# Loads of a retention-plus-feed-forward kernel issued in another order around its attention stretches

## The chip, the cores and the metric

The kernel runs on one core of a Trainium2 chip. Five engines work side by side, each through its own list of instructions in a fixed order: TensorE (PE, with its weight loads shown as PEld), VectorE (DVE), ScalarE (ACT), GpSimd (POOL) and SyncE (SP). SP does nothing here but issue transfers between the chip's main memory and the on-chip buffers: if one transfer must wait, every transfer behind it in SP's list waits too. The metric is the device time of one execution in microseconds (us); lower is better.

## The reference, cut to what matters

```python
scores = matmul(q, k.T) / sqrt(64)                  # q, k, v: 8 batches, 8 heads, 576 positions, 64 wide
ret    = matmul(scores * decay_per_head, v)         # decay gamma**(i-j) below the diagonal, 0 above
x      = ret as (4608 tokens, 512)
h      = x @ w_in                                   # 512 x 2048
out    = (h - tanh(h)) @ w_out                      # 2048 x 512
```

## The kernel before, in words

The 576 positions are cut into nine blocks of 64 positions, and a block n is worked on for all eight batches at once: 512 tokens. Retention is computed block by block with a running state. For two batches of a block (a turn) the function `attend` runs 128 small matmuls (64x64) on PE. The `attend` of one turn also computes the scores of the next one, so a turn's q and k (tile `qk`) must be loaded and q multiplied by a decay table (tile `qtab` or `work`, by POOL, `prep`) before the previous turn's `attend`; its v and rows of k (tile `vr`) must be loaded and v scaled (POOL again) before its own.

The feed-forward part is done in words: each fp32 operand is split into a high and a low word, and three fp32r matmuls replace one. `mm1(n, f)` computes one of 16 slices f of the hidden layer of block n, `mm2(n, f)` multiplies slice f by the second weight: 12 matmuls of 128x512. A hidden slice is written to main memory (`spill`) and read back (`fetch`, tile `s`, three buffers) some slices ahead of its `mm2`; ACT makes its high word `gh`, DVE its low word `gl` (`split`; for every third slice the tiles are `gs`).

The order of the program is:

- A first part converts the weights and does `mm1` of blocks 0 and 1.
- The late loop (k = 0 to 31) does `mm2` of blocks 1 and 0. `late[k + 4]` is fetched in step k, `resume` makes its tanh two steps later, `words` its words. In the same loop DVE makes sums of the first weight's slices (`sums`), ACT and SP store them to `wvar`, and `raw_words` stores 24 unchanged words of those slices (256 KB each), one per step for k = 6 to 29.
- A loop over f = 0 to 15 does `mm1(2, f)`.
- `stage_b(n, m0)` does `mm2` of an even block n (2, 4, 6, 8), f = 0 to 15. Before each even f it runs one `attend` of the turns of blocks n+1 and n+2: `attend(m0)` to `attend(m0 + 7)`. Here `attend(i)` means the i-th of the eight in its stage (0 to 7), on PE ahead of `mm2(n, 2i)`. At its end `attend` prepares tables (`prep_turn`) and issues the loads of coming turns (`load_turn`).
- `stage_a(n)` does the first matmul of two blocks with seven products in place of eight, from sums of x (tiles `xhv`, `xlv`, made by `put`) and the sums of weights in `wvar`, which `load_slot` brings in (tile `ws`, four products at a time). Stage B and stage A alternate: B(2), A(3), B(4), A(5), B(6), A(7), B(8).

Two tables of q (for two blocks) are loaded by `load_tables` into a part of tile `work`. A load into it may not start before POOL's last `prep` with the old tables has ended. The order of each engine's list is the order in which the code issues its instructions; nothing reorders it afterwards (`in_order`).

The lines of the profile that matter below: L297 the small matmuls, L445 `mm1`, L500 `mm2`, L898 the products of stage A, L929 `mm2` inside stage A; L470 `fetch`, L693 `raw_words`, L724 sums to `wvar`, L769 `load_tables`, L788 `load_turn`, L887 `load_slot`; L247 `prep` on POOL; L475 `resume`, L482 `words`, L913 and L914 `split`, L814 `put` of low words on DVE.

Of the kernel before, what the change touches and what calls it, by code (L numbers as in the profile page):

```python
# [9 lines left out]
F32 = mybir.dt.float32  # L10
F32R = mybir.dt.float32r
# [8 lines left out]
P = 128  # L20
NF = DF // P
# [16 lines left out]
FIRST = 3  # L38
# [33 lines left out]
def retention_ffn(ctx: ExitStack, tc: tile.TileContext, ins, out, spill, wvar):  # L72
    nc = tc.nc
# [392 lines left out]
    fetched = {}  # L466

    def fetch(n, f):
        fetched[n, f] = pool.tile([P, BLK], F32, tag="g", bufs=3, name=f"s{n}_{f}")
        nc.sync.dma_start(fetched[n, f], spill[n, f])  # L470
# [265 lines left out]
    for k, (n, f) in enumerate(late):  # L736
        if k in (3, 16, 29):
            follow, scale = entry3(first + (0, 2, 5)[(3, 16, 29).index(k)], rest)
        if 0 < k < len(late) - 1:
            words(*late[k + 1])  # L740
        if k < len(late) - 2:
            resume(*late[k + 2])
        if k + 4 < len(late):
            fetch(*late[k + 4])
        if k in (3, 16, 29):

            follow()
# [12 lines left out]
        if 6 <= k < 30:  # L760
            raw_words(*raws[k - 6])

    turns = [(c + u) * B + b for c in range(FIRST, NC, 2) for b in range(0, B, 2) for u in range(2)]
    def load_tables(c):

        both = work[:, 2].rearrange("p (n i s) -> p n i s", n=2, i=4)
        nc.sync.dma_start(both, qtab_d[c - 1 : c + 1].rearrange("n p i s -> p n i s"))  # L769
        for u in range(2):  # L770
            qtabs[c + u] = both[:, u]

    def load_turn(m, t):
        if m >= len(turns):
            return
        j = turns[m]
        c, b = divmod(j, B)
        if m == 1 and t == 0:
            load_qtab(c)
        if t == 0 and m and m % 8 == 0:  # L780
            load_tables(c)
# [6 lines left out]
        nc.sync.dma_start(part, qkv_d[c - 1, b : b + 2, :, 2 * t : 2 * t + 2].rearrange("u p t i s -> p u t i s"))  # L788
        parts[j, t] = part
        for u in range(2):  # L790
            loaded.setdefault(j + u, Parts([None, None])).parts[t] = part[:, u]

    def prep_turn(m, t):
        if m < len(turns):
            prep(turns[m], t)


# [10 lines left out]
    def put(v, b, src, sub):  # L808

        hi, lo = [x[:, :, b * C : (b + 2) * C].rearrange("p i (u t) -> p u i t", u=2) for x in xv[v]]  # L810
        if sub == 0:
            nc.scalar.copy(hi, src)
        else:
            nc.vector.tensor_tensor(lo, src, hi.bitcast(F32), op=ALU.subtract)  # L814
# [3 lines left out]
    def attend(m, between):  # L818

        j = turns[m]  # L820
        c, b = divmod(j, B)
        first, states = (c - FIRST) % 2 == 0, c < NC - 1
        if first and b == 0:
            new_xv()
        o = bank(f"own{j}", "own")
        outs, same = pair(m_out, j, o), []
        if states:
            new = bank(f"new{j}", "new")
            same += pair(m_state, j, new)
        more = m + 1 < len(turns)  # L830
        if more:
            sc = bank(f"s{turns[m + 1]}", "h")
            same = pair(m_score, turns[m + 1], sc) + same
        run(same, outs)
        if more:
            after_score(turns[m + 1], sc, 2)
        if first:
            a = pool.tile([P, 2, 4, C], F32, tag="cv", bufs=4, name=f"xa{j}")
            kept[b] = a
            put(0, b, o[:, :, 0:2], 0)  # L840
            put(5, b, o[:, :, 2:4], 0)
            nc.scalar.copy(a, o)
            if states:
                add_state(j, new)
            between()
            put(0, b, a[:, :, 0:2], 1)
            put(5, b, a[:, :, 2:4], 1)
        else:
            a = kept.pop(b)
            t13 = pool.tile([P, 2, 2, 2, C], F32, tag="cv", bufs=4, name=f"t13_{j}")  # L850
            t24 = pool.tile([P, 2, 2, 2, C], F32, tag="cv", bufs=4, name=f"t24_{j}")
            t1, t3, t2, t4 = t13[:, 0], t13[:, 1], t24[:, 0], t24[:, 1]
            own = pool.tile([P, 2, 4, C], F32, tag="cv", bufs=4, name=f"xb{j}")
            nc.scalar.copy(own, o)
            put(4, b, o[:, :, 2:4], 0)
            nc.vector.tensor_tensor(t3, own[:, :, 2:4], own[:, :, 0:2], op=ALU.subtract)
            nc.gpsimd.tensor_tensor(t2, t3, a[:, :, 0:2], op=ALU.add)
            nc.vector.tensor_tensor(t1, own[:, :, 0:2], a[:, :, 0:2], op=ALU.subtract)
            nc.gpsimd.tensor_tensor(t4, a[:, :, 2:4], t2, op=ALU.subtract)
            if states:  # L860
                add_state(j, new)
            put(3, b, t3, 0)
            put(2, b, t1, 0)
            between()
            put(4, b, own[:, :, 2:4], 1)
            put(3, b, t3, 1)
            put(2, b, t1, 1)
            put(1, b, t2, 0)
            put(6, b, t4, 0)
            put(1, b, t2, 1)  # L870
            put(6, b, t4, 1)
        prep_turn(m + 2, 0)
        prep_turn(m + 1, 1)
        load_turn(m + 3, 0)
        load_turn(m + 2, 1)


    slots = {}
    per = NV * NPAIR // 4

    def load_slot(n):

        if n >= per * ((NC - FIRST) // 2):
            return
        w = pool.tile([P, 4, 2, 2, P], F32R, tag=("xh0", "xh1", "xl0")[n % 3], bufs=1, name=f"ws{n}")
        at = 4 * (n % per)
        nc.sync.dma_start(w.bitcast(F32).rearrange("p v s c m -> p v (s c m)"), wvar[:, at : at + 4])  # L887
        slots[n] = w

    count = [0]  # L890

# [13 lines left out]
    def split(n, f, g, spare):  # L905

        if spare:
            both = const.tile([P, 2, BLK], F32R, tag=place_of(2), name="gs")
            gh, gl = both[:, 0], both[:, 1]
        else:  # L910
            gh = pool.tile([P, BLK], F32R, tag="gh", name=f"gh{n}_{f}")
            gl = pool.tile([P, BLK], F32R, tag="gl", name=f"gl{n}_{f}")
        nc.scalar.copy(gh, g)  # L913
        nc.vector.tensor_tensor(gl, g, gh.bitcast(F32), op=ALU.subtract)  # L914
        gs[n, f] = (gh, gl)
# [20 lines left out]
    def stage_a(na):  # L936
# [44 lines left out]
        for f in range(2):  # L981
            split(nb, f, fetched.pop((nb, f)), False)

    def stage_b(n, m0):

        for f in range(NF):
            def ahead():
                if f + 3 < NF:
                    fetch(n, f + 3)
                if f + 2 < NF:  # L990
                    split(n, f + 2, fetched.pop((n, f + 2)), f % 3 == 0)

            if f % 2 == 0 and n < NC - 1:
                attend(m0 + f // 2, ahead)
            else:
                ahead()
            if (n, f) != (NC - 1, NF - 2):
                mm2(n, f)
            if n == 2 and f in (7, 9, 11):
                load_slot((f - 7) // 2)  # L1000


    for f in range(NF):
        mm1(2, f)
        if f == 0:
            mm2(*late[-1])
        if f == 1:
            scale()
        for _ in range(2):
            next(summed, None)  # L1010
        if f == 8:
            load_turn(1, 0)
            load_turn(2, 0)
            load_turn(1, 1)
        if f == 11:
            prep_turn(1, 0)
        if 11 < f < 15:
            fetch(2, f - 12)
    assert next(summed, 0) == 0
    work = pool.tile([P, 4, DM], F32, tag="xl1", bufs=1, name="work")  # L1020
    load_tables(FIRST)
    for f in range(2):
        split(2, f, fetched.pop((2, f)), False)
    stage_b(2, 0)
    for s in range((NC - FIRST) // 2):
        stage_a(FIRST + 2 * s)
# [59 lines left out]
```

## Time and profile before

| | |
|---|---|
| time, median of 3 runs | 874.08 us (873.55 to 874.1) |
| the profiled execution | 872.58 us, of which the span from first to last instruction is 870.8 us |
| TensorE busy / granted clock over the span | 848.8 us (97%) / 0.995 |
| transfers | 174.67 MB, mean 201 GB/s |

A row of the timeline reads: start, duration, engine, line, operation, output tile <- input tiles, shapes, count, and in brackets how long the engine stood idle before it and what it waited for. SPq rows are issues of transfers. A row of the waits reads: who waited, on what; us in total, times, longest. A row of the windows reads: the stretch, its length, busy time of PE, PEld, DVE, ACT and POOL with instruction counts, granted TensorE clock (1.00 is full, 0.50 half), share of the DMA engines, GB/s. The profile lists PE's waits for its own instructions as "issue", and the transfers that bring those instructions as a queue of the kind "instruction", one packet of 16 KB each on queue q8.

### The profile page before, as it was taken

The page shows a single profiled execution, that of the slowest core. Times are in us where ns is not written, and L with a number is a line of the kernel's source. Part 1 is how long each engine was busy: PE and PEld are TensorE (multiplying, and loading weights), DVE is VectorE, ACT ScalarE, POOL GpSimd, SP SyncE. Part 2 cuts the span into 40 slices and gives each one's busy share as a digit, 9 for nine tenths or more (in the row PEclk, how much of TensorE's full clock was granted, in tenths as well). Part 3 has the DMA queues.
Part 4 walks back from the last instruction along what each step waited for, and adds up shares of the span by engine and source line. Part 5 has one row for each costly group of instructions (what it writes and reads, how often), then busy time and mean ns, then how long its engine had stood idle before and what let it go on. Part 6 is the DMA issues. An engine that isn't in the chain of part 4 may idle for free.

```text
span 870.8 us, 18540 instructions
## 1 busy us (share of the span) xinstructions
PE 848.8 (97%) x7701; PEld 699.0 (80%) x7702; DVE 499.7 (57%) x774; ACT 340.1 (39%) x633; POOL 155.4 (18%) x133
## 2 busy tenths in 40 slices
PE   7999999999998899999999999999999999999997
PEld 6788888877886787888888888888887888888886
DVE  5989778758565756444437675343447654343321
ACT  4887665544333233322333333232343333232321
POOL 0001001010002423111223342121315212121100
PEclk9999999999999999999999999999999999999999
DMA  8976956886586668453557466444575355352432
GB/s 311 378 238 217 354 172 215 238 307 238 194 289 239 218 207 264 173 193 120 193 183 238 165 202 222 148 167 149 180 239 186 122 169 176 139 183 83 136 108 72
DMA packets 69652, 174.67 MB, mean 201 GB/s; under 512 B 7488, under 2 KB 8896, under 8 KB 64192
## 3 DMA queue, kind: packets, MB, share of 16 engines
q1 hardware_dynamic: 69040, 172.57, 58.8%
q8 instruction: 60, 0.98, 0.4%
q10 hardware_dynamic: 528, 0.92, 0.3%
q14 instruction: 24, 0.20, 0.1%
HBM read 124.70 MB, written 48.76 MB: 199 GB/s over the span
## 4 chain that ended last, share of the span: by engine, by line
PE 89%; DMA 5%; DVE 3%; ACT 2%; issue 1%; SPq 0%; POOL 0%; DVEq 0%; ACTq 0%; POOLq 0%
PE o L500 26%; PE o L929 15%; PE h L445 15%; PE pv L898 7%; PE pnew L898 7%; PE py L898 4%; PE pz L898 4%; PE pown L898 4%; DMA s<-spill_dram 3%; PE s L297 3%; PE own L297 3%; PE new L297 2%; DMA rwi<-in_w_in_dram 1%; DMA a<-in_first_dram 1%; DVE xlv L814 1%
## 5 line engine op out<-in xcount | busy, mean ns | idle before, releaser
L500 PE MATMUL o<-wo,gh 128*128 128x512 f32 x608 | 156.6, 394 | 3.4 <-ACT gh L482 2.4
L500 PEld LDWEIGHTS o<-wo,gh 128*128 128x128 f32 x608 | 112.4, 188 | 29.6 <-ACT gh L482 3.8
L952 POOL TENSOR_TENSOR c<-c,th 128x512 f32<-128x512 f32 x48 | 62.1, 1297 | 267.4 <-ACT th L948 266.3
L948 ACT ACTIVATE th<-c 128x512 f32<-128x512 f32 x72 | 45.5, 632 | 149.1 <-DVE c L962 98.3
L445 PE MATMUL h<-xh,wi 128*128 128x512 f32 x384 | 97.7, 392 | 1.4 <-ACT wi L152 0.6
L445 PEld LDWEIGHTS h<-xh,wi 128*128 128x128 f32 x384 | 71.4, 188 | 17.4 <-ACT wi L152 1.1
L500 PE MATMUL o<-wo,gl 128*128 128x512 f32 x304 | 84.2, 389 | 0.0
L929 PE MATMUL o<-wo,gs 128*128 128x512 f32 x288 | 70.7, 389 | 0.0
L500 PEld LDWEIGHTS o<-wo,gl 128*128 128x128 f32 x304 | 57.1, 188 | 12.0
L247 POOL TENSOR_TENSOR vr<-vr,vtab 128x512 f32<-128x512 f32 x27 | 33.1, 1228 | 178.0 <-DMA vr<-in_qkv_dram 178.0
L929 PEld LDWEIGHTS o<-wo,gs 128*128 128x128 f32 x288 | 54.1, 188 | 11.2
L500 PE MATMUL o<-wo,gs 128*128 128x512 f32 x240 | 61.1, 403 | 0.0
L898 PE MATMUL pnew<-xhv,ws 128*128 128x512 f32 x192 | 59.5, 391 | 0.3
L297 PE MATMUL own<-qk,vr 64*64 64x64 f32 x928 | 57.7, 221 | 2.1 <-issue 1.5
L898 PE MATMUL pv<-xhv,ws 128*128 128x512 f32 x192 | 59.1, 389 | 0.0
L297 PE MATMUL own<-qk,state 64*64 64x64 f32 x928 | 58.6, 223 | 0.0
L500 PEld LDWEIGHTS o<-wo,gs 128*128 128x128 f32 x240 | 45.6, 193 | 10.0
L958 DVE TENSOR_TENSOR work<-pown,work 128x512 f32<-128x512 f32 x24 | 16.6, 690 | 63.0 <-PE pown L898 63.0
L445 PE MATMUL h<-xl,wi 128*128 128x512 f32 x192 | 51.6, 390 | 0.0
L914 DVE TENSOR_TENSOR gl<-s,gh 128x512 fp32r<-128x512 f32 x44 | 32.4, 744 | 29.3 <-ACT gh L913 17.5
L929 PE MATMUL o<-wo,gh 128*128 128x512 f32 x192 | 48.9, 389 | 0.0
L297 PEld LDWEIGHTS own<-qk,vr 64*64 64x64 f32 x928 | 47.4, 137 | 1.6 <-issue 0.9
(147 smaller groups left out, 1590.8 us busy)
## 6 DMA issues: line engine op xcount, KB each, us to landing
ws<-wvar_dram SPq DMA_DIRECT2D x42, 1024.0 KB, 4.7
s<-spill_dram SPq DMA_DIRECT2D x94, 256.0 KB, 4.0
qk<-in_qkv_dram SPq DMA_DIRECT2D x29, 512.0 KB, 4.6
vr<-in_qkv_dram SPq DMA_DIRECT2D x29, 512.0 KB, 6.2
spill_dram<-c SPq DMA_DIRECT2D x48, 256.0 KB, 2.3
spill_dram<-g SPq DMA_DIRECT2D x36, 256.0 KB, 3.4
rwi<-in_w_in_dram SPq DMA_DIRECT2D x16, 512.0 KB, 5.6
rwo<-in_w_out_dram SPq DMA_DIRECT2D x16, 512.0 KB, 4.9
```

The costliest lines, as they stand in the source:

```text
L247: nc.gpsimd.tensor_tensor(a, a, table, op=ALU.mult)
L297: nc.tensor.matmul(out_, w, x, start=start, stop=stop)
L445: nc.tensor.matmul(hp, win[f][:, cc // 2, a, cc % 2 * P : (cc % 2 + 1) * P], x[:, cc, :], start=(k == 0), stop=(k == 3 * NCC - 1))
L500: nc.tensor.matmul(ops[n][t], g[:, t * P : (t + 1) * P], wout[f_][:, a, :], start=(f_ == first and k == 0), stop=(f_ == final and k == 2),)
L814: nc.vector.tensor_tensor(lo, src, hi.bitcast(F32), op=ALU.subtract)
L898: nc.tensor.matmul(into, w[:, a, k], x[:, k], start=start and i == 0, stop=i == len(terms) - 1, skip_group_check=not start,)
L914: nc.vector.tensor_tensor(gl, g, gh.bitcast(F32), op=ALU.subtract)
L929: nc.tensor.matmul(ops[n][t], g[:, t * P : (t + 1) * P], wout[f][:, a, :], start=(j == 0 and f == fs[0] and k == 0), stop=last_,)
L948: nc.scalar.activation(th, c, AF.Tanh)
L952: nc.gpsimd.tensor_tensor(c, c, tanh(c), op=ALU.subtract)
L958: nc.vector.tensor_tensor(u2, y, u2, op=ALU.add)
```

## The change

Five edits, all in the order of work; the arithmetic is the same.

1. `raw_words`: two per step for k = 4 to 8, one for k = 9 to 14, none for 15 to 18 and 20, one for 19 and 21 to 27.
2. In the loop of `mm1(2, f)`, turn 2's q is loaded at f = 2 and prepared at f = 6 with the table of block 3 that is still loaded; turn 1's loads follow at f = 6 and its preparations at f = 9 and 10; slices 0 to 2 of block 2 are fetched one f earlier, and slices 0 and 1 are split at f = 14 and 15 instead of behind the loop. `load_tables(3)` moves from before stage B(2) into its `attend(1)`.
3. In every stage B the fetch of slice f+3 is issued behind `attend` (and so behind its loads) instead of inside it.
4. In stage B(2) the first three weight slots are loaded as six halves of 512 KB at f = 0, 2, 4, 8, 10, 12 instead of three whole ones at f = 7, 9, 11.
5. In the odd `attend`s the low words are made on DVE in the order 2, 1, 3, 4, 6 instead of 4, 3, 2, 1, 6.

```diff
@@ late loop
-        if 6 <= k < 30:
-            raw_words(*raws[k - 6])
+        for _ in range(2 if 4 <= k < 9 else k in (9, 10, 11, 12, 13, 14, 19, 21, 22, 23, 24, 25, 26, 27)):
+            raw_words(*raws.pop(0))
@@ load_turn
-        if t == 0 and m and m % 8 == 0:
+        if t == 0 and m and m % 8 == 0 or (m, t) == (4, 0):
             load_tables(c)
@@ prep_turn: each (m, t) is prepared once
-        if m < len(turns):
+        if m < len(turns) and (m, t) not in prepared:
+            prepared.add((m, t))
             prep(turns[m], t)
@@ attend, odd
             between()
-            put(4, b, own[:, :, 2:4], 1)
-            put(3, b, t3, 1)
-            put(2, b, t1, 1)
             put(1, b, t2, 0)
             put(6, b, t4, 0)
+            put(2, b, t1, 1)
             put(1, b, t2, 1)
+            put(3, b, t3, 1)
+            put(4, b, own[:, :, 2:4], 1)
             put(6, b, t4, 1)
@@ stage_b
+    halves_at = (0, 2, 4, 8, 10, 12)
             def ahead():
-                if f + 3 < NF:
-                    fetch(n, f + 3)
                 if f + 2 < NF:
                     split(n, f + 2, fetched.pop((n, f + 2)), f % 3 == 0)
...
                 attend(m0 + f // 2, ahead)
             else:
                 ahead()
+            if f + 3 < NF:
+                fetch(n, f + 3)
+            if n == 2 and f in halves_at:
+                load_slot(*divmod(halves_at.index(f), 2))
             if (n, f) != (NC - 1, NF - 2):
                 mm2(n, f)
-            if n == 2 and f in (7, 9, 11):
-                load_slot((f - 7) // 2)
@@ loop of mm1(2, f)
-        if f == 8:
-            load_turn(1, 0)
+        if f == 2:
             load_turn(2, 0)
+        if f == 6:
+            prep_turn(2, 0)
+            load_turn(1, 0)
             load_turn(1, 1)
-        if f == 11:
-            prep_turn(1, 0)
-        if 11 < f < 15:
-            fetch(2, f - 12)
+        if f in (9, 10):
+            prep_turn(1, f - 9)
+        if 10 < f < 14:
+            fetch(2, f - 11)
+        if f > 13:
+            split(2, f - 14, fetched.pop((2, f - 14)), False)
     work = pool.tile([P, 4, DM], F32, tag="xl1", bufs=1, name="work")
-    load_tables(FIRST)
-    for f in range(2):
-        split(2, f, fetched.pop((2, f)), False)
     stage_b(2, 0)
```

`load_slot(n, part)` loads the half `part` of slot n where a part is given.

What this does to SP's list shows at three places. First the late loop, steps k = 16 to 19, behind the store of block 1's output (`out_0`). `s0_5` is slice 5 of block 0; rows with `wi` are raw words. Before:

```order
L525 DMA out_0_dram<-ob1_2057 64x4x512 x2
L693 DMA wvar_dram<-wi6_534 128x512
L470 DMA s0_4_2192<-spill_dram 128x512
L219 DMA vr21_2194<-in_qkv_dram 128x2x512
L233 DMA one23_2196<-in_qkv_dram 128x1024
L693 DMA wvar_dram<-wi6_534 128x512
L470 DMA s0_5_2223<-spill_dram 128x512
L693 DMA wvar_dram<-wi7_562 128x512
L470 DMA s0_6_2246<-spill_dram 128x512
```

The same place now:

```order
L525 DMA out_0_dram<-ob1_2064 64x4x512 x2
L470 DMA s0_4_2198<-spill_dram 128x512
L219 DMA vr21_2200<-in_qkv_dram 128x2x512
L233 DMA one23_2202<-in_qkv_dram 128x1024
L470 DMA s0_5_2228<-spill_dram 128x512
L470 DMA s0_6_2250<-spill_dram 128x512
```

Two raw words (512 KB) no longer stand between the output and slice 5. They stand earlier, two in a step.

Second, SP's list where the loop of `mm1(2, f)` ends and stage B(2) begins; `work` is the pair of tables, `qk34` and `vr26` the first loads of `attend(0)`, `ot7` the last sums. Before:

```order
L724 DMA wvar_dram<-ot7_3018 128x1024
L769 DMA work_3045<-in_qtab_dram 128x2x256
L470 DMA s2_3_3142<-spill_dram 128x512
L788 DMA qk34_3151<-in_qkv_dram 128x2x512
L788 DMA vr26_3153<-in_qkv_dram 128x2x512
L470 DMA s2_4_3171<-spill_dram 128x512
```

The same place now:

```order
L724 DMA wvar_dram<-ot7_3022 128x1024
L789 DMA qk34_3148<-in_qkv_dram 128x2x512
L789 DMA vr26_3150<-in_qkv_dram 128x2x512
L470 DMA s2_3_3152<-spill_dram 128x512
L893 DMA ws0_3154<-wvar_dram 128x1024
L470 DMA s2_4_3176<-spill_dram 128x512
```

The tables are gone from here, slice 3 has moved behind `qk34` and `vr26`, and a half of a weight slot has come in.

Third, SP's list around `attend(5)` of stage B(2), where the tables of the next two blocks are loaded. Before:

```order
L788 DMA qk38_3647<-in_qkv_dram 128x2x512
L788 DMA vr30_3649<-in_qkv_dram 128x2x512
L470 DMA s2_12_3663<-spill_dram 128x512
L887 DMA ws1_3680<-wvar_dram 128x2048
L470 DMA s2_13_3762<-spill_dram 128x512
L769 DMA work_3045<-in_qtab_dram 128x2x256
L788 DMA qk40_3778<-in_qkv_dram 128x2x512
L788 DMA vr38_3780<-in_qkv_dram 128x2x512
L470 DMA s2_14_3794<-spill_dram 128x512
L887 DMA ws2_3812<-wvar_dram 128x2048
```

The same place now:

```order
L789 DMA qk38_3648<-in_qkv_dram 128x2x512
L789 DMA vr30_3650<-in_qkv_dram 128x2x512
L470 DMA s2_11_3652<-spill_dram 128x512
L893 DMA ws1_3407<-wvar_dram 128x1024
L470 DMA s2_12_3670<-spill_dram 128x512
L770 DMA work_3055<-in_qtab_dram 128x2x256
L789 DMA qk40_3778<-in_qkv_dram 128x2x512
L789 DMA vr38_3780<-in_qkv_dram 128x2x512
L470 DMA s2_13_3782<-spill_dram 128x512
L893 DMA ws2_3784<-wvar_dram 128x1024
```

Slice 13 stood ahead of the tables and now stands behind them and behind both loads of the coming turns. The same holds for stage B(4), without the weight slots; stage B(6) loads no tables, and stage B(8) has no `attend`.

More of the change, by code (lines that the diff above doesn't have):

```diff
@@ L759, in retention_ffn @@
             mm2(n, f)
-        if 6 <= k < 30:
-            raw_words(*raws[k - 6])
+        for _ in range(2 if 4 <= k < 9 else k in (9, 10, 11, 12, 13, 14, 19, 21, 22, 23, 24, 25, 26, 27)):
+            raw_words(*raws.pop(0))
+    assert not raws
     turns = [(c + u) * B + b for c in range(FIRST, NC, 2) for b in range(0, B, 2) for u in range(2)]
@@ L791, in load_turn @@
             loaded.setdefault(j + u, Parts([None, None])).parts[t] = part[:, u]
+    prepared = set()
     def prep_turn(m, t):
-        if m < len(turns):
+        if m < len(turns) and (m, t) not in prepared:
+            prepared.add((m, t))
             prep(turns[m], t)
@@ L879, in retention_ffn, with load_slot @@
     per = NV * NPAIR // 4
-    def load_slot(n):
+    def load_slot(n, part=None):
         if n >= per * ((NC - FIRST) // 2):
             return
[L885 to L888, printed above, removed]
+        if n not in slots:
+            slots[n] = pool.tile([P, 4, 2, 2, P], F32R, tag=("xh0", "xh1", "xl0")[n % 3], bufs=1, name=f"ws{n}")
+        at = slice(0, 4) if part is None else slice(2 * part, 2 * part + 2)
+        to = slots[n].bitcast(F32).rearrange("p v s c m -> p v (s c m)")[:, at]
+        nc.sync.dma_start(to, wvar[:, 4 * (n % per) + at.start : 4 * (n % per) + at.stop])
     count = [0]
@@ L1010, in retention_ffn @@
             next(summed, None)
-        if f == 8:
+        if f == 2:
+            load_turn(2, 0)
+        if f == 6:
+            prep_turn(2, 0)
             load_turn(1, 0)
-            load_turn(2, 0)
             load_turn(1, 1)
-        if f == 11:
-            prep_turn(1, 0)
-        if 11 < f < 15:
-            fetch(2, f - 12)
+        if f in (9, 10):
[4 more added lines that the diff above has]
+            split(2, f - 14, fetched.pop((2, f - 14)), False)
     assert next(summed, 0) == 0
     work = pool.tile([P, 4, DM], F32, tag="xl1", bufs=1, name="work")
-    load_tables(FIRST)
-    for f in range(2):
-        split(2, f, fetched.pop((2, f)), False)
     stage_b(2, 0)
```

## The prediction

> **What bounds the kernel now.** I read the page first, then the windows by stage, then PE's waits inside the stages that the change touches.
>
> ```profile
> PE 848.8 (97%) x7701; PEld 699.0 (80%) x7702; DVE 499.7 (57%) x774; ACT 340.1 (39%) x633; POOL 155.4 (18%) x133
> 223.00:265.00 42.00, 42.00 (x306) 34.83 (x304) 25.42 (x47) 13.01 (x23) 1.77 (x1) 1.00 0.72 251
> 265.00:336.00 71.00, 64.36 (x1104) 52.83 (x1097) 45.25 (x67) 23.62 (x54) 25.66 (x23) 0.95 0.68 234
> 457.00:519.00 62.00, 61.32 (x1194) 51.00 (x1185) 44.90 (x68) 22.61 (x52) 24.80 (x22) 1.00 0.65 205
> 640.00:702.00 62.00, 61.16 (x1028) 50.91 (x1020) 42.67 (x65) 22.58 (x52) 21.35 (x19) 1.00 0.49 159
> ```
>
> PE is the bound; no edit removes a matmul, so only PE's idle time and slow clock can move. The windows are most of the loop of `mm1(2, f)`, where PE is never idle, and stages B(2), B(4), B(6). B(2) has the same work as B(4) and takes 71 us against 62: some 9 us are the most that B(2) can give. The waits of PE in 120 to 345 us (first six rows), in B(4) and in B(6) (last two):
>
> ```profile
> PE new L297 <- issue: 3.0, 1, 3.0
> PE o L500 <- ACT gh L482: 2.4, 2, 1.3
> PE s L297 <- POOL qk L247: 2.1, 1, 2.1
> PE o L500 <- ACT gh L913: 0.9, 1, 0.9
> PE pown L898 <- DVE xlv L814: 0.6, 1, 0.6
> PE own L297 <- POOL vr L247: 0.5, 1, 0.5
> PE own L297 <- issue: 0.7, 1, 0.7
> PE own L297 <- issue: 0.8, 1, 0.8
> ```
>
> All that can be won in waits is here. The clock adds to it:
>
> ```profile
> 275.30:278.70 3.40, 3.40 (x106) 3.19 (x99) 0.78 (x3) 0.63 (x2) 0.00 (x0) 0.50 0.76 276
> 301.20:304.40 3.20, 0.19 (x15) 0.05 (x4) 2.77 (x5) 0.00 (x0) 0.94 (x1) 1.00 0.44 172
> 306.00:309.40 3.40, 3.40 (x10) 2.62 (x9) 1.36 (x3) 0.75 (x2) 0.00 (x0) 0.50 0.78 211
> 496.80:497.70 0.90, 0.23 (x16) 0.10 (x8) 0.27 (x1) 0.00 (x0) 0.00 (x0) 1.00 0.00 0
> ```
>
> Twice PE ran 3.4 us at clock 0.50, losing 1.7 us each time: soon after the waits of 2.1 and 0.5 us (which lie close together) and after that of 3.0. The waits of 0.7 to 1.3 us left the clock at 1.00.
>
> **The change part by part.** The sum is made against the profiled execution, 872.58 us, 1.5 us below the median of 874.08 to which I then apply it.
>
> *Raw words earlier.* The two L482 waits end with a late slice:
>
> ```profile
> s<-spill_dram SPq DMA_DIRECT2D x1, 256.0 KB, 7.3
> 180.26 1.98 PE L500 MATMUL o<-wo,gh 128*128 128x512 f32 x8
> 182.32 0.63 ACT L475 ACTIVATE th<-s 128x512 f32<-128x512 f32 x1 [2.76 <-DMA s<-spill_dram]
> 184.44 0.74 PE L500 MATMUL o<-wo,gh 128*128 128x512 f32 x2 [1.30 <-ACT gh L482]
> 196.85 0.50 PE L500 MATMUL o<-wo,gh 128*128 128x512 f32 x1 [1.14 <-ACT gh L482]
> q1 hardware_dynamic: 859, 2.43, 78.1%
> ```
>
> The first row is the slice issued at 175.0. The last row is a congested stretch, 293.3 to 302.1 us: 2.43 MB in 8.8 us, so 256 KB cost 0.95 us there. Two raw words fewer ahead of that slice are 1.9 us, more than 1.30: this wait goes. The second wait has one raw word fewer ahead (0.95 us), but PE arrives 1.3 us earlier while part of the queue behind it (sums, a `qk`) is moved by DVE's progress and comes earlier too; I credit 0.9 of 1.14. Gain 2.2; ends 0 (the congestion only moves) and 2.4. In steps 4 to 8 each slice now has one more raw word in each step ahead of it, 2.85 us for three transfers in a step of 12 matmuls (8 take 1.98, so just under 3 us); cost nothing, covered by the two steps between fetch and `resume`. If that cover is gone, each late slice costs about 1 us.
>
> *Turn 2's q, tables and splits.*
>
> ```profile
> 272.57 1.26 POOL L247 TENSOR_TENSOR qk<-qk,work 128x512 f32<-128x512 f32 x1 [19.58 <-DMA work<-in_qtab_dram]
> 273.89 0.32 PE L297 MATMUL s<-qk 64*64 64x64 f32 x3 [2.09 <-POOL qk L247]
> 263.00:265.20 2.20, 2.10 (x128) 1.96 (x128) 1.00 0.88 307
> 273.80:278.10 4.30, 3.60 (x128) 3.28 (x128) 0.68 0.92 329
> ```
>
> POOL had stood 19.6 us until `work` landed; PE's `attend(1)` then waited 2.1 for that q and 0.5 for the `vr` prepared behind it, and ran 3.60 us of small matmuls where `attend(0)` needed 2.10 (the two last rows, L297 alone). With q prepared at f = 6 from the table already there, both waits and the slow clock go; with slices 0 and 1 split at f = 14 and 15, the 0.9 of L913 goes. Gain 2.1 + 0.5 + 0.9 + 1.7 = 5.2; ends 4.0 (another small wait takes a place) and 5.2. The moved loads (three of 512 KB, one table) pass only stores, in the stretch where PE is busy 42 of 42 us; they cost nothing; were one late at `attend(0)`, PE would wait out its lateness. SP also loses its wait for the last sums ahead of `work`.
>
> *The loads behind each stretch, and halves.* The 3.0 us "issue" is PE out of instructions:
>
> ```profile
> q8 instruction: 1, 0.02, 2.5%
> ```
>
> The 2.43 MB of 293.3 to 302.1 us were data alone, a whole 1 MB weight slot among them. This row is 302.1 to 304.5: one packet of instructions; PE resumes at 304.4. So the packet stood behind the data that SP had issued behind `attend(3)`. Now that burst is `qk`, `vr` and two slices, 1.5 MB without a slot, which at 277 GB/s is 3.8 us less than before. The packet asked for in `attend(2)`'s burst meets a half more. I take 3.0 + 1.7 (clock) down to 0.7, the size that such waits have in B(4) and B(6), where bursts are of this size: gain 4.0; ends 4.7 and, if the half hits the other packet, 0.8. In B(4) and B(6) both slices now stand in the burst at once instead of one 2 us later; +0.3 for the packets there, ends 0 and 1.9 (0.95 each). SP's issues of six halves in place of three slots cost it some 0.4 us each and delay nobody who waits.
>
> The Trainium skill says otherwise: Runtime: NRT & Kernel Launch, section Instruction fetch mechanics, has instructions refilled in blocks of 16 KiB, ahead of use, with the crossing mostly hidden. The row above, with a packet of that size and PE idle until it had come, does not agree. By that rule this term would be 0.
>
> *Slice 13 behind the tables.* This edit costs. SP waits for POOL before it loads new tables (B(2) and B(4)):
>
> ```profile
> SPq L769 <- POOL qk L247: 10.6, 1, 10.6
> SPq L769 <- POOL qk L247: 9.2, 1, 9.2
> 502.81 0.38 SPq L769 DMA_DIRECT2D work<-in_qtab_dram  x1
> 503.28 0.42 SPq L788 DMA_DIRECT2D qk<-in_qkv_dram  x1
> 503.75 0.46 SPq L788 DMA_DIRECT2D vr<-in_qkv_dram  x1
> 504.31 0.89 SPq L470 DMA_DIRECT2D s<-spill_dram  x2
> 510.26 0.62 ACT L913 CAST gs<-s 128x512 fp32r<-128x512 f32 x1 [3.10 <-DMA s<-spill_dram]
> 508.76 1.98 PE L500 MATMUL o<-wo,gh 128*128 128x512 f32 x8
> 327.38 0.62 ACT L913 CAST gs<-s 128x512 fp32r<-128x512 f32 x1 [4.10 <-DMA s<-spill_dram]
> 324.90 1.98 PE L500 MATMUL o<-wo,gh 128*128 128x512 f32 x8
> ```
>
> Before, the first slice behind the tables was 14, and ACT could split it at 510.26 in B(4) and 327.38 in B(2). Now the slice in that place, behind the same 1.25 MB and the same wait for POOL, is 13, and `mm2(n, 13)` began at 508.76 and 324.90. It cannot start before ACT's 0.62 is done: 510.9 and 328.0. PE waits 2.1 and 3.1 us. What frees SP is POOL's `prep` behind `attend(5)`, and the change moves nothing ahead of it. Ends of each wait: 0, and 4 with a half slot or a packet in the way. The clock comes on top: idle times of 3.0 us and of 2.1 with 0.5 close by were followed by 3.4 us at 0.50, those up to 1.3 by none; 3.1 and 2.1 are nearest to the former, so 1.7 each. Cost 2.1 + 3.1 + 3.4 = 8.6; ends 0 and 10.4.
>
> The Trainium skill, TensorE: Matmul & The Clock Gate, section HAM oscillation, gives "no PE-idle gaps >~3.4µs" as the rule. The idle of 3.0 and of 2.1 with 0.5 us did slow the clock here, so the trace does not agree. By the rule this cost would be 5.2.
>
> For the other odd slices the same move is covered: they land behind 1 MB of loads instead of ahead, and `mm2` asks for them one `attend` and three `mm2` (2.1 and three times just under 3, about 10 us) after the burst. If a burst took over 9 us, each would cost its excess.
>
> *Order of low words.*
>
> ```profile
> 334.30 3.90 DVE L814 TENSOR_TENSOR xlv<-t,xhv 128x256 fp32r<-128x256 f32 x4
> ```
>
> Stage A's second product waited 0.6 for the third of these four; it now comes second of five: gain 0.6, ends 0 and 0.6.
>
> **Sum:** -2.2 - 5.2 - 4.0 + 0.3 + 8.6 - 0.6 = -3.1 us, 0.36% of 874.08: 871.0 us.
>
> **The rivals.**
>
> - *The new waits stay short of the slow clock.* The idle of 1.3 us kept its clock, and nothing between 1.3 and 2.1 was seen. Then 8.6 becomes 5.2: -6.5, 867.6 us. For it: B(4)'s 2.1 us is alone, not joined by 0.5. This is also what the skill's rule on idle gaps would give.
> - *Slice 13 is not late at all*, because the tables are freed earlier or the transfers behind them run faster. Against it: the wait for POOL ended alike in both stages, and the same transfers stand ahead. -3.1 - 8.6 = -11.7: 862.4 us.
> - *Slower: instruction packets stand behind whole bursts.* In `attend(2)` of B(2) the half adds 512 KB, 1.9 us, and the second slice in a burst 0.95. If a packet waits for everything in the burst, PE waits 1.9 + 0.3 there and loses 1.7 of clock: of the 4.7 only 0.8 is won. In B(4) and B(6) 0.95 each is added, and one of the two, 0.8 + 0.95 = 1.75, slows the clock: +3.6 in place of +0.3. Then -2.2 - 5.2 - 0.8 + 3.6 + 8.6 - 0.6 = +3.4: 877.5 us. It decides from about 512 KB that go ahead of a packet. For it: 2.43 MB went ahead of the one at 302. Against: half of it was one whole slot, which is not in that burst any more.
> - *The change does not do what it says for the instructions:* the 3.0 us stays where it is, being bound to a place in PE's list. -3.1 + 4.0 = +0.9: 875.0 us, no change. The skill's rule on hidden refills would give this too.
>
> **How the numbers follow.** About 0.2%, 1.75 us, is what can be told from no change. Chances: forecast 0.53, short of the slow clock 0.16, slice 13 in time 0.08, whole bursts 0.13, issue wait stays 0.10. The forecast's own range is -6 to 0 us (868 to 874): late loop 1 to 2.4, packets 3 to 4.7, tables 7 to 9; 0.40 of its 0.53 is beyond -1.75, 0.11 within, 0.02 above. Faster: 0.40 + 0.16 + 0.08 = 0.64; same: 0.11 + 0.10 = 0.21; slower: 0.13 + 0.02 = 0.15. The range 865.0 to 877.0 leaves out slice 13 in time and most of the whole bursts, about 0.18.
>
> **What would show it.** Late loop: PE's waits on L482 near 0.3 instead of 2.4. Opening: no wait of L297 on POOL's `qk`, clock 1.00 in `attend(1)`. Bursts: no "issue" wait over 1.5 us in B(2), whose window falls to about 67 us. Tables: a new wait of PE L500 on ACT L913 of 2 to 3 us each in B(2) and B(4), behind `attend(6)`, with clock 0.50 after it, and B(4) longer than 62 by about 4. I am wrong if B(4) keeps its 62 us (then -11.7 is near), or if B(2) still shows issue waits above 2 us.

## The result, and the profile after

The changed kernel takes 880.9 us (median of 7 runs, 877.41 to 882.91) against 874.08 (median of 7, 871.68 to 876.12): a ratio of 1.0076, with a 95% interval of 1.0052 to 1.0099. It is slower by 6.8 us; the forecast was 871.0 us and a range of 865 to 877. The profiled execution after took 878.19 us, span 876.4, against 872.58 and 870.8: 5.6 us of the difference are in the two traces.

Numbers of lines below the turns' loads have moved: an attend's copies into `xa` and `xb` are L846 and L858 (before L842, L854), DVE's difference L860 (L856), POOL's `t` L861 (L857), the tables' load L770 (L769), the split L918 and L919 (L913, L914). L247, L297, L482, L500 are as they were.

First the windows of the kernel after: the loop of `mm1(2, f)`, then B(2), B(4) and B(6), each from the first matmul of `attend(0)` to the first product of stage A. Columns: stretch, its length, busy time of PE, weight loads, DVE, ACT and POOL, granted clock, share of the DMA engines, GB/s.

```profile
223.00:265.00 42.00, 42.00 (x305) 34.81 (x304) 27.02 (x48) 15.38 (x28) 4.09 (x3) 1.00 0.76 256
261.30:333.00 71.70, 64.60 (x1217) 52.99 (x1217) 44.02 (x69) 23.69 (x54) 23.09 (x21) 0.98 0.68 238
453.20:520.80 67.60, 64.03 (x1217) 52.62 (x1217) 45.15 (x68) 22.96 (x52) 24.90 (x22) 0.97 0.59 191
641.00:707.70 66.70, 64.14 (x1057) 53.16 (x1057) 42.15 (x65) 23.14 (x53) 21.23 (x19) 0.97 0.47 150
```

Cut at the same two events, these three stages took 72.2, 62.8 and 62.8 us before. B(2) gained 0.5; B(4) and B(6) lost 4.8 and 3.9. PE's waits after, in B(2) (first four), B(4) (next three) and B(6) (last two); the columns are the total, the count, the longest:

```profile
PE s L297 <- POOL qk L247: 2.2, 2, 1.5
PE own L297 <- POOL vr L247: 1.7, 2, 1.0
PE o L500 <- issue: 1.5, 1, 1.5
PE o L500 <- ACT gh L918: 1.5, 1, 1.5
...
PE o L500 <- ACT gh L918: 2.3, 1, 2.3
PE own L297 <- issue: 1.0, 1, 1.0
PE own L297 <- POOL vr L247: 0.3, 1, 0.3
...
PE own L297 <- POOL vr L247: 1.3, 3, 0.7
PE s L297 <- POOL qk L247: 1.1, 1, 1.1
```

What the edits were to remove has gone: the issue wait of 3.0 us, the waits of `attend(1)` on `qk` and `vr`, those on the first split and on the low words; of the 2.4 us on L482 in the late loop 1.6 are left. An issue wait of 1.5 us stands at another place of B(2), in the `mm2` behind `attend(3)`. The wait on slice 13 has come: 2.3 us in B(4), 1.5 in B(2). The rest was not forecast: POOL's `qk` and `vr` are late again, now for `attend(2)` and `attend(6)` of B(2) and for `attend(2)` of B(6), a stage in which no tables are fetched and no slot is loaded. Three times PE ran 3.4 us at clock 0.50, from 315.1, 509.7 and 659.9 us, once in each stage.

**Where that comes from.** ACT's list in B(6) after, behind `attend(0)`, and what DVE, POOL and PE made of it:

```profile
644.21 0.64 ACT L918 CAST gs<-s 128x512 fp32r<-128x512 f32 x1
651.85 0.62 ACT L918 CAST gh<-s 128x512 fp32r<-128x512 f32 x1 [7.00 <-DMA s<-spill_dram]
652.38 0.58 ACT L858 COPY xb<-own 128x512 f32<-128x512 f32 x1
652.51 0.69 DVE L919 TENSOR_TENSOR gl<-s,gh 128x512 fp32r<-128x512 f32 x1 [6.26 <-ACT gh L918]
653.12 0.68 DVE L309 TENSOR_TENSOR qk<-s,mask 128x512 f32<-128x512 f32 x1
653.72 0.41 DVE L860 TENSOR_TENSOR t<-xb 128x256 f32<-128x256 f32 x1
654.21 0.85 POOL L861 TENSOR_TENSOR t<-t,xa 128x256 f32<-128x256 f32 x1 [21.20 <-DVE t L860]
655.84 1.71 POOL L247 TENSOR_TENSOR qk<-qk,work 128x512 f32<-128x512 f32 x1
657.61 0.33 PE L297 MATMUL s<-qk 64*64 64x64 f32 x3 [1.14 <-POOL qk L247]
```

and the same place before:

```profile
645.82 0.62 ACT L913 CAST gh<-s 128x512 fp32r<-128x512 f32 x1 [2.63 <-DMA s<-spill_dram]
649.22 0.59 ACT L854 COPY xb<-own 128x512 f32<-128x512 f32 x1 [2.78 <-DMA s<-spill_dram]
649.84 0.43 DVE L856 TENSOR_TENSOR t<-xb 128x256 f32<-128x256 f32 x1 [0.92 <-DMA s<-spill_dram]
650.35 0.86 POOL L857 TENSOR_TENSOR t<-t,xa 128x256 f32<-128x256 f32 x1 [19.00 <-DVE t L856]
651.98 1.74 POOL L247 TENSOR_TENSOR qk<-qk,work 128x512 f32<-128x512 f32 x1
654.73 0.27 PE L297 MATMUL s<-qk 64*64 64x64 f32 x2
```

ACT does its list in order. The split of slice 3 stands in it ahead of `attend(1)`'s copy of `own` into `xb`. Before, the slice had come ahead of the turns' loads and was split at 645.82, long before that copy was wanted. After, it lands behind 1 MB of q, k and v; ACT stands 7.0 us in front of it and splits it at 651.85, when `attend(1)` has been over on PE since 650.8. Counted from the start of `attend(0)` (641.0 after, 639.3 before) the split begins at 10.8 instead of 6.5 us, 4.4 later; the 2.8 that ACT had to spare before the copy take up that much of it, and the copy starts 1.6 us after its matmuls instead of at once. (The row of the copy before names a transfer as what it waited for; it began when `attend(1)`'s matmuls ended, at 649.1.) The Trainium skill, PSUM — Partial Sum Buffer, section Engine vs sequencer instructions, calls ScalarE's queue a strict first-in, first-out one, and these rows agree. DVE is held by the same split: its low word `gl` waits for `gh` until 652.51, and the mask on `attend(1)`'s scores (L309) and the difference (L860) stand behind it in DVE's list. So the difference starts 1.3 us after the start of the copy that it reads, instead of 0.6. POOL's `t` waits for the difference, and POOL's `prep` for the turn after stands behind `t`. From the end of `attend(1)` to POOL's `t` it is 3.4 us instead of 1.2, 2.2 more: 1.5 by ACT's list and 0.7 by DVE's. Before, `qk` was ready at 651.98 + 1.74 = 653.72 and asked for at 654.73: 1.0 us of slack. 2.2 - 1.0 is the 1.14 that PE waits for `qk`; `vr`, next on POOL, adds 0.72.

### The profile page after: what moved, and what is told of

Same layout as the page of the kernel before. It is cut to its first block, busy times and chain, and to the rows that moved or that the text cites. A ratio compares the mean times of both kernels' runs of the same rounds, so it can differ in the third digit from the quotient of the medians.

```text
span 876.4 us, 18543 instructions
## 1 busy us (share of the span) xinstructions
PE 850.9 (97%) x7701; PEld 700.2 (80%) x7702; DVE 496.6 (57%) x774; ACT 340.7 (39%) x633; POOL 154.7 (18%) x133
## 4 chain that ended last, share of the span: by engine, by line
PE 78%; DMA 8%; DVE 6%; ACT 3%; issue 2%; POOL 2%; SPq 1%; ACTq 0%; DVEq 0%; POOLq 0%
PE o L500 18%; PE o L934 15%; PE h L445 14%; PE pnew L903 7%; PE pv L903 7%; DMA s<-spill_dram 7%; PE pown L903 4%; PE py L903 4%; PE pz L903 4%; PE own L297 2%; PE s L297 2%; PE new L297 1%; DVE xlv L818 1%; DMA rwi<-in_w_in_dram 1%; DVE s L476 1%
## 5 line engine op out<-in xcount | busy, mean ns | idle before, releaser
L500 PE MATMUL o<-wo,gh 128*128 128x512 f32 x608 | 158.8, 398 | 6.8 <-ACT gh L918 3.8
L500 PEld LDWEIGHTS o<-wo,gh 128*128 128x128 f32 x608 | 113.4, 190 | 34.0 <-ACT gh L918 4.9
L500 PE MATMUL o<-wo,gl 128*128 128x512 f32 x304 | 85.0, 392 | 0.0
L934 PE MATMUL o<-wo,gs 128*128 128x512 f32 x288 | 70.6, 389 | 0.0
L919 DVE TENSOR_TENSOR gl<-s,gh 128x512 fp32r<-128x512 f32 x44 | 32.4, 741 | 63.2 <-ACT gh L918 46.7
L500 PEld LDWEIGHTS o<-wo,gl 128*128 128x128 f32 x304 | 57.6, 190 | 12.2
L247 POOL TENSOR_TENSOR vr<-vr,vtab 128x512 f32<-128x512 f32 x27 | 33.1, 1226 | 174.0 <-DMA vr<-in_qkv_dram 89.0
L297 PE MATMUL own<-qk,vr 64*64 64x64 f32 x928 | 58.4, 223 | 4.4 <-POOL vr L247 3.3
L918 ACT CAST gh<-s 128x512 fp32r<-128x512 f32 x44 | 27.3, 623 | 86.7 <-DMA s<-spill_dram 72.5
L500 PE MATMUL o<-wo,gs 128*128 128x512 f32 x240 | 59.2, 394 | 0.0
L297 PE MATMUL own<-qk,state 64*64 64x64 f32 x928 | 59.1, 224 | 0.0
L500 PEld LDWEIGHTS o<-wo,gs 128*128 128x128 f32 x240 | 44.4, 188 | 9.6
L297 PEld LDWEIGHTS own<-qk,vr 64*64 64x64 f32 x928 | 47.9, 138 | 4.4 <-POOL vr L247 4.1
```

The lines of the kernel that those rows point to most:

```text
L247: nc.gpsimd.tensor_tensor(a, a, table, op=ALU.mult)
L297: nc.tensor.matmul(out_, w, x, start=start, stop=stop)
L500: nc.tensor.matmul(ops[n][t], g[:, t * P : (t + 1) * P], wout[f_][:, a, :], start=(f_ == first and k == 0), stop=(f_ == final and k == 2),)
L934: nc.tensor.matmul(ops[n][t], g[:, t * P : (t + 1) * P], wout[f][:, a, :], start=(j == 0 and f == fs[0] and k == 0), stop=last_,)
```

## The experiments

A time is the median as measured; the ratio behind it is to the kernel before, measured beside it on the same chip, with its 95% interval in brackets. Chips differ a little, so gains and losses in microseconds are the ratio's, taken on 874.

**The fetch back inside `attend`.** The changed kernel with one edit undone.

```diff
             def ahead():
+                if f + 3 < NF:
+                    fetch(n, f + 3)
                 if f + 2 < NF:
...
-            if f + 3 < NF:
-                fetch(n, f + 3)
             if n == 2 and f in halves_at:
```

> The changed kernel with one edit undone: the fetch of slice f + 3 stands inside attend again, ahead of its loads; everything else of the change is kept. Theory A (an odd slice that lands behind the 1 MB of loads holds ACT, which must split it before it copies what the next attend has left in own; that makes POOL's prep late and PE's attend after that waits): the POOL waits (2.2 and 1.7 us in B(2), 0.3 in B(4), 1.3 and 1.1 in B(6)), the waits for slice 13 (1.5 and 2.3) and the slow clock behind them (1.7 each, three times) go. B(4) and B(6), 67.6 and 66.7 us from attend(0) to the next stage, fall to the 62.7 they had before, and B(2) by 5 to 7 us: 880.9 - 8.9 - 6 = 866 us (863 to 869), so 1% faster than before. Rival B (only slice 13 behind the tables costs): 880.9 - 2.3 - 1.7 - 1.5 = 875.4, B(6) stays at 66.7. Rival C (the size of the bursts and the instruction packets in them, which the place of a fetch in the burst does not alter): 880, unchanged.

Measured: 860.0 us, 0.986 [0.984, 0.988]. Its windows of B(2), B(4), B(6):

```profile
259.90:323.80 63.90, 61.92 (x1217) 51.31 (x1217) 43.30 (x69) 24.13 (x54) 23.10 (x21) 1.00 0.78 267
444.10:506.80 62.70, 62.02 (x1218) 51.69 (x1218) 45.21 (x68) 22.79 (x52) 24.81 (x22) 1.00 0.64 205
627.00:689.50 62.50, 61.89 (x1057) 51.58 (x1057) 42.57 (x65) 23.07 (x53) 21.14 (x19) 1.00 0.50 160
```

B(4) and B(6) are back at what they were before the change; no wait on POOL is left in any of the three, and the clock is 1.00. The rivals fall: slice 13 alone would have given 875, the size of the bursts 880. The change without this one edit is 1.4% faster than the kernel before, and is the best version found. It gained some 4 us more than I expected: 7.8 of the 18.2 between the two spans (876.4 and 858.2) are in B(2), where I had 6, and 1.3 lie outside the three stages.

**That edit alone, on the kernel before.**

```diff
             def ahead():
-                if f + 3 < NF:
-                    fetch(n, f + 3)
...
+            if f + 3 < NF:
+                fetch(n, f + 3)
             if (n, f) != (NC - 1, NF - 2):
                 mm2(n, f)
```

> The kernel before with that one edit alone: the fetch of slice f + 3 stands behind attend and its loads; nothing else is changed. Theory A: POOL's prep is late behind the odd attends in all of B(2), B(4) and B(6), and slice 13 is late: B(4) 62.7 to about 67.6, B(6) 62.8 to about 66.7, B(2) longer by 2 to 6: 874.1 + 8.8 + 4 = 887 us (882 to 890). Rival B (slice 13 alone): B(2) and B(4) longer by 3 to 5 each, B(6) as before, 880 to 883. Rival C (bursts and packets as the changed kernel makes them, with the halves): no more than 876, since the halves and the earlier loads are not here.

Measured: 887.5 us, 1.0163 [1.0139, 1.0186]. The waits in B(4), where before there was one issue wait of 0.7:

```profile
PE o L500 <- ACT gh L913: 2.8, 1, 2.8
PE s L297 <- POOL qk L247: 1.4, 1, 1.4
PE new L297 <- issue: 1.0, 1, 1.0
PE own L297 <- POOL vr L247: 0.7, 1, 0.7
```

B(2), B(4) and B(6) take 77.8, 71.6 and 65.4 us: 5.6, 8.8 and 2.6 more than before. So the moved fetch needs neither the halves nor the opening to do its harm, and B(6), which loads no tables, is longer too: neither rival fits (880 to 883 with B(6) as before, and no more than 876).

**Slice 13 alone ahead of the loads.** The changed kernel, in which `ahead` fetches for f = 10 and the fetch behind `attend` leaves that one out.

```diff
             def ahead():
+                if f == 10:
+                    fetch(n, f + 3)
...
-            if f + 3 < NF:
+            if f + 3 < NF and f != 10:
                 fetch(n, f + 3)
```

> The changed kernel, in which slice 13 alone is fetched ahead of the loads behind attend(5) and so ahead of the new tables; all other odd slices stay behind the loads. Theory A: the wait of mm2(n, 13) for ACT goes (2.3 us in B(4) with 1.7 of slow clock, 1.5 in B(2)), the POOL waits stay: 880.9 - 5.5 = 875.4 us (874 to 878), B(6) stays at 66.7. Rival B (slice 13 is all of the cost): the same as the run with every fetch inside attend, both near 875. Rival C: 880.

Measured: 874.0 us, 1.0015 [1.0001, 1.003], and B(2), B(4), B(6) 69.9, 64.5 and 65.9 us. The waits in B(2) (first three) and B(6):

```profile
PE s L297 <- POOL qk L247: 2.3, 2, 1.1
PE o L500 <- ACT gh L918: 1.4, 1, 1.4
PE own L297 <- POOL vr L247: 1.4, 2, 0.7
...
PE own L297 <- POOL vr L247: 1.4, 2, 0.7
PE s L297 <- POOL qk L247: 1.2, 1, 1.2
```

B(4)'s wait on a slice is gone, and in B(2) slice 15 is late by 1.4 instead. The waits on POOL stay. So slice 13 is one part of the loss and not the whole of it: this run and the first, which rival B had alike, are 1.6% apart.

**An odd slice split one step later.** All loads as in the changed kernel; what moves is the high word in ACT's list and, with it, the low word in DVE's. At odd f nothing is split; the next `attend` does both splits at the place where it did one.

```diff
-            def ahead():
+            def ahead(f=f):
...
+            def both():
+                if f > 0:
+                    ahead(f - 1)
+                ahead()
-            if f % 2 == 0 and n < NC - 1:
-                attend(m0 + f // 2, ahead)
-            else:
-                ahead()
+            if n == NC - 1:
+                ahead()
+            elif f % 2 == 0:
+                attend(m0 + f // 2, both)
```

> The changed kernel, all loads as they are, but ACT splits an odd slice one step later: inside the next attend, behind its copies of own and of t3 and t1 and just ahead of the even slice's split. Nothing that POOL's prep needs is behind the split any more. Theory A: the waits of L297 on POOL go (2.2 and 1.7 us in B(2), 0.3 in B(4), 2.4 in B(6)) with two stretches of slow clock (1.7 each), some 9 us: 872 us (869 to 875), while slice 13 is still late in B(4) by about 2.3, since the tables stand ahead of it. Rival B (slice 13 alone) and rival C (bursts and packets): 880 or a little more, since the bytes and their order are unchanged.

Measured: 871.8 us, 0.9977 [0.9963, 0.9991]. The place in B(6) that was shown above:

```profile
648.73 0.59 ACT L858 COPY xb<-own 128x512 f32<-128x512 f32 x1 [5.99 <-PE own L297]
649.85 0.86 POOL L861 TENSOR_TENSOR t<-t,xa 128x256 f32<-128x256 f32 x1 [18.96 <-DVE t L860]
650.45 1.15 ACT L918 CAST gh<-s 128x512 fp32r<-128x512 f32 x2
```

ACT's copy now waits for PE and for nothing else, POOL's `t` comes 1.1 us behind it (1.8 in the changed kernel), and B(6) takes 62.8 us as it did before the change. The bytes, their order and the bursts are those of the changed kernel; 8.6 us of its time (1.0076 - 0.9977, give or take 0.27%) hung on the place of the split in the lists of ACT and DVE; no run parts the two engines. This is the run that shows the mechanism: `mm2` itself waits for a late slice by more than 0.5 us at slice 13 alone. There it stands as forecast, here `mm2(n, 13)` of B(2) and of B(4):

```profile
318.22 1.03 PE L500 MATMUL o<-wo,gh 128*128 128x512 f32 x3 [3.04 <-ACT gh L918]
506.14 2.46 PE L500 MATMUL o<-wo,gh 128*128 128x512 f32 x6 [2.12 <-ACT gh L918]
```

and the clock behind each wait:

```profile
319.00:322.40 3.40, 3.40 (x9) 2.64 (x8) 1.36 (x3) 0.62 (x1) 0.00 (x0) 0.50 0.95 360
506.70:510.10 3.40, 3.40 (x9) 2.65 (x8) 1.47 (x4) 0.62 (x1) 0.00 (x0) 0.50 0.51 192
```

**Both cures at once**: slice 13 ahead of the loads, and the odd splits later.

> The changed kernel with both partial cures at once: slice 13 fetched ahead of the loads, and an odd slice's split behind the next attend's copies; all other odd slices are still fetched behind the loads. With the split moved alone (871.8 us) PE still waited 3.0 us in B(2) and 2.3 in B(4) for slice 13 and ran twice 3.4 us at clock 0.50 (1.7 each). Theory A (late POOL and late slice 13 are all that the moved fetch costs): these 8.7 us go, 863 us (861 to 866), close to the 860 of the run with every fetch inside attend. Rival (something else of the moved fetch costs too, such as larger bursts ahead of packets of instructions): 868 or more.

Measured: 864.9 us, 0.9914 [0.9896, 0.9932]; B(2), B(4), B(6) 65.5, 63.0 and 62.8 us, clock 1.00 throughout. On 874 that is 866.5 us (864.9 to 868.1), at the upper end of theory A, and the interval just reaches the rival's 868: most of the cost is found, not all. Late POOL and late slice 13 together are 1.6% of the 2.2% between the changed kernel and the one with the fetch inside. The last 0.5% is only partly placed: 1.6 us of 3.5 between the two spans are in B(2), where splits are still waited for (0.6, 0.5 and 0.2 us), 0.6 in B(4) and B(6); the rest lies outside these stages, where the two programs are alike.

**The other edits, one by one, on the kernel before.** The opening (turn 2's q, the tables, the first splits), by its lines in the change's diff:

> The kernel before with the opening edit alone: q and k, tables of turn 2 and the first splits early, one table for turn 4 fetched behind attend(1). Everything else as before. If that edit is worth the sum of the waits it removes (2.1 + 0.5 for L297 on POOL, 0.9 for L913, 1.7 of slow clock): -5.2 us, 867 to 870, ratio 0.994, with the issue wait of 3.0 us and its slow clock still in B(2). Rival: another wait takes its place at the start of B(2), as the move of loads makes the bursts of attend(0) and attend(1) larger (the table now stands in them): -2 or less.

Measured: 867.1 us, 0.9933 [0.9913, 0.9952], that is -5.9. B(2) takes 66.8 instead of 72.2 us; its issue wait (2.9) and the slow clock after it, the window below, are still there.

```profile
298.90:302.30 3.40, 3.40 (x10) 2.63 (x9) 1.71 (x4) 1.36 (x4) 0.00 (x0) 0.51 0.68 173
```

The raw words two in a step:

> The kernel before with the raw words alone stored two in a step early on. If the term of the forecast holds, the waits on L482 fall from 2.4 to 0.3: -2.2, ratio 0.9975. The trace of the run with the fetch inside attend shows three such waits left of 0.3 to 0.8 us, and so the rival: about 1.3 gained, ratio 0.9985, hardly to be told from no change.

Measured: 870.0 us, 0.9975 [0.996, 0.999], that is -2.2. The waits on L482 fall to 1.1 in its trace; a short new one comes at 143 us, where the words are stored in twos. So the time agrees with the forecast, the trace shows a little over half of it, and the interval (-0.9 to -3.5) cannot tell the forecast from the rival's 1.3.

The slots in halves behind the loads, with the fetch where it was:

> The kernel before with the weight slots alone loaded in six halves, each behind the loads of an attend and ahead of mm2, instead of in three wholes behind mm2. If the issue wait of 3.0 us in B(2) comes from the whole slot ahead of the packet of instructions: it falls to 2 or less and its slow clock of 1.7 goes: -2.5 to -4.0 us, ratio 0.996. Rival (the wait is bound to the place in PE's list, not to the slot): ratio 1.000. Rival (a half in attend(2)'s burst holds another packet there, and a half in attend(5)'s holds slice 13 or 14): up to 1.002.

Measured: 871.7 us, 0.9981 [0.9965, 0.9997], that is -1.7. B(2) takes 69.0 us. The wait of 3.0 us at `attend(4)` is down to 0.2, and one of 2.5 has come in the `mm2` behind `attend(3)`:

```profile
PE o L500 <- issue: 2.5, 1, 2.5
PE new L297 <- issue: 0.2, 1, 0.2
```

That is the packet that comes in at the end of `attend(2)`'s burst, which now has a half in it. The third part of the expectation came: the stall moved to the other packet.

**The half taken out of that burst**, in the kernel with the fetch inside `attend`.

```diff
-    halves_at = (0, 2, 4, 8, 10, 12)
+    halves_at = (0, 2, 8, 10, 12, 14)
```

> The kernel with the fetch inside attend (860 us) and the halves of the slots behind attend 0, 1, 4, 5, 6, 7 instead of 0, 1, 2, 4, 5, 6. It has 1.9 us of issue wait in the mm2 that stands behind attend(2), where a half of 512 KB goes ahead of the packet of instructions. If the half holds the packet, that wait falls to 0.3 or less: 858 to 859 us. Rival (the two slices and q, k, v in the burst hold it): 860, unchanged. The half behind attend(7) goes into no slice's way and is not needed before stage A's ninth product.

(The wait of 1.8 us stands in the `mm2` behind `attend(3)`; its packet comes in at the end of `attend(2)`'s burst.) Measured: 861.2 us, 0.9868 [0.984, 0.989], no different from 860.0. That wait is gone from the list, and `attend(4)` waits 1.2 for the next packet where it had waited 0.2:

```profile
PE new L297 <- issue: 1.2, 1, 1.2
```

B(2) takes 63.5 us against 63.9. Moving 512 KB from one burst to another again moved the stall.

## Why the prediction was wrong

By its own steps; measured sizes are from the runs of single edits.

- *Raw words:* -2.2 forecast, -2.2 measured (interval -0.9 to -3.5), so close partly by luck. The mark set for it, 0.3 us of waits left, was not met: 1.6 are left in the changed kernel, 1.1 with the edit alone.
- *Opening:* -5.2 forecast, -5.9 measured (-4.2 to -7.6). Right.
- *Bursts and halves:* -4.0 forecast; the halves alone gave -1.7 (-0.3 to -3.1). Mis-sized: I had named the lower end, 0.8, for the case that the half holds the other packet, and that case came. What the fetch adds to it cannot be parted from the fetch's own cost. The issue wait did not stay in its place. The +0.3 for packets in B(4) and B(6) did not come either, and still less the slower rival's +3.6: their issue waits are 1.0 and none, after 0.7 and 0.8.
- *Low words:* the wait of 0.6 is gone in the trace after; not run alone, being too small to time.
- Without the fetch behind the loads, the forecast's own terms sum to -2.2 - 5.2 - 4.0 - 0.6 = -12.0. The run without it gave -12.2 (-10.6 to -14.0). So far the sum held, but not term by term: the three edits that were run alone gave -2.2, -5.9 and -1.7, with 0.6 for the low words -10.4, so that the near hit is in part luck.
- *Slice 13:* +8.6 forecast, as waits of 3.1 and 2.1 us and twice 1.7 of clock. With the splits moved, the trace shows just this: 3.0 and 2.1, and twice 3.4 us at 0.50. As time it was too large: the two pairs of runs that differ in slice 13's place alone are 5.3 us apart (1.0076 and 1.0015, give or take 2.4) and 5.5 (0.9977 and 0.9914, give or take 2.0). For the first pair the trace of the changed kernel has the same, 1.5 + 2.3 and one 1.7 of clock; the two traces of the second are 8.7 apart, and why its medians give less is not shown. By its own terms the upper end was twice 4 and 3.4, 11.4, and not 10.4. In the changed kernel the wait in B(2) is 1.5 only, because POOL is late and PE later: the tables are asked for 7.1 us after `attend(5)` has ended on PE (306.23 to 313.36) instead of 4.6 (314.30 to 318.92). The step said that the change moves nothing ahead of the `prep` that frees SP; it moves the `xb` copy and DVE's difference behind it.
- *The step that failed:* "For the other odd slices the same move is covered", with the cost nothing. I asked when `mm2` wants the slice, some 10 us after the burst, and `mm2` did get them in time. I did not ask what stands behind the split in the lists of ACT and DVE. In ACT's the first instruction is the copy of the next attend's `own`, wanted as soon as that attend has ended. The two rows of B(6) before show it: split at 645.82, copy at 649.22, so the cover was 3.4 us less the 0.62 of the split, and not 10; and POOL's `qk` had 1.0 us to spare behind that. From the changed kernel to the one with only the odd splits moved it is 8.6 us, which I had put at nothing. It alone turns the forecast of -3.1 into +5.5; measured +6.8. That this comes so close is again partly luck: slice 13 cost some 3 us less than its term, and 4.7 us of the moved fetch (0.9914 against 0.986) are in no term.

None of the rivals was this. The slower one had the right stages, B(4) and B(6), and the nearest time (877.5 against 880.9), but by another mechanism: waits for packets, of which B(6) after has none in its list.

## What to carry to other kernels

A transfer that is moved behind others is not covered until its consumer's consumer needs it: it is covered until an engine that must touch it reaches it in its list, and everything behind it on that engine is then late too. Read, in the rows of each such engine, what comes next behind the waiting instruction and how much slack its product has downstream; here it was 2.8 us on ACT and 1.0 on POOL, where the count to the matmul gave 10. When a load must come late, move its first touch behind the work that others wait for: that alone was worth 1%, and leaving the load early 2%.

## What the runs showed of the hardware

**What slows the clock is the share of a fixed window, not the length of a wait.** The stretches at 0.50 begin on a grid of 3.413 us: those of the changed kernel at 315.11, 509.67 and 659.85 us, 57 and 44 steps apart; those before at 275.31 and 306.03, 9 steps. Each follows a window of this grid in which PE was busy for less than half of it. The windows ahead of those three (the third holds the waits of 1.14 and 0.72 on POOL):

```profile
311.70:315.11 3.41, 1.20 (x49) 0.87 (x52) 3.41 (x5) 0.40 (x1) 2.81 (x2) 1.00 0.08 24
506.26:509.67 3.41, 1.13 (x5) 0.84 (x5) 1.00 (x2) 1.65 (x4) 1.91 (x2) 1.00 1.03 365
656.44:659.85 3.41, 1.55 (x85) 1.39 (x88) 3.41 (x3) 0.62 (x1) 3.41 (x3) 1.00 0.16 56
```

The one ahead of 306.03 in the kernel before:

```profile
302.62:306.03 3.41, 1.60 (x29) 1.36 (x30) 2.04 (x4) 0.93 (x3) 0.00 (x0) 1.00 0.07 20
```

The most idle windows seen that slowed nothing, each in its own run's grid; with the halves alone:

```profile
271.48:274.90 3.42, 1.62 (x8) 1.00 (x6) 0.00 (x0) 0.26 (x1) 0.90 (x1) 1.00 0.73 189
```

and with the raw words alone:

```profile
298.44:301.85 3.41, 1.75 (x105) 1.61 (x104) 3.41 (x5) 0.00 (x0) 2.26 (x2) 1.00 0.82 333
301.85:305.26 3.41, 2.27 (x32) 1.91 (x33) 1.37 (x3) 1.60 (x4) 0.00 (x0) 1.00 0.14 25
```

PE busy for 1.60 us of 3.41 was followed by 0.50, 1.62 was not. The last two rows are one issue wait of 2.8 us that fell across a border and cost no clock; in the kernel before its like, 3.0 us, fell 1.2 and 1.8 and did. So, as an estimate from these rows, a wait between about 1.8 us (3.41 less 1.60, all in one window) and 3.6 (twice that, over two) costs 1.7 more or not, by where it falls in the grid, and the clock differs from run to run (0.989 to 0.996 over the span in the seven runs of the changed kernel); my rule by the nearest wait could not see it. The busy time alone is not the whole rule: in the run of the raw words alone a window already at 0.50, with PE busy for 2.71 us, was followed by a second one at 0.50 (274.54 us), and in the run of the half taken out a window near the program's start, with 1.89 us, was followed by one too (11.06 us). Why is open. The Trainium skill, TensorE: Matmul & The Clock Gate, section What's actually happening, has such a window, free-running, of 3413 ns; the starts agree with it. That section of the Trainium skill has the clock slowed after an idle window; here windows were enough in which PE worked up to 1.60 us.

**Packets of instructions are late beside the data of a burst**, and 512 KB decided which one. In the four variants of the halves the issue waits of B(2) were 3.0 (before), 2.5 + 0.2 (halves alone), 1.8 + 0.2 (with the opening and the raw words) and 1.2 (half moved); none removed them. The record does not show when a packet is asked for; that the data hold it is read from where the stall goes when they move.
